# Heads p and p + 4 as a pair: q and k loaded over 128 partitions in one transfer

## The chip, the core and the metric

The kernel runs on one core of one Trainium2 chip. A core has five engines that run side by side, each with its own queue that it works off in order: PE (TensorE: matmuls and, on its weight port PEld, weight loads), DVE (VectorE), ACT (ScalarE), POOL (GpSimd) and SP (SyncE, which here issues most of the DMAs). Sixteen DMA engines move data between DRAM and the on-chip memory SBUF, which has 128 partitions. PE writes its results to PSUM.

The metric is the device time of one execution in microseconds (us), here the median of several runs. A profiled execution gives the trace. "Span" is the time from the program's first to its last instruction in that execution.

## What is computed

Eight batches of eight heads of attention with a forget gate, over 576 tokens with 64 dimensions each, and behind it a bilinear feed-forward layer on the rows of all heads side by side. Everything comes in and goes out as float32.

```python
batch, n_heads, seq, head_dim = (8, 8, 576, 64)
...
n_tokens, d_model, d_ff = (4608, 512, 1536)
...
def _attn_ref(q, k, v, f) -> np.ndarray:
    B, H, S, D = q.shape
    scale = 1.0 / np.sqrt(D)
    scores = scale * np.matmul(q, k.transpose(0, 1, 3, 2))
    log_f = np.log(np.clip(f, 0.0001, 1.0))
    cum = np.cumsum(log_f, axis=-1)
    decay = cum[:, :, :, None] - cum[:, :, None, :]
    causal = np.triu(np.ones((S, S), dtype=bool), k=1)
    scores = np.where(causal, -1000000000.0, scores + decay)
    scores = scores - np.max(scores, axis=-1, keepdims=True)
    attn = np.exp(scores)
    attn = attn / (np.sum(attn, axis=-1, keepdims=True) + 1e-09)
    return np.matmul(attn, v).astype(np.float32)
...
def _moe_ref(x, w_a, w_b, w_out) -> np.ndarray:
    a = x @ w_a
    b = x @ w_b
    return (a * b @ w_out).astype(np.float32)
...
    x = np.ascontiguousarray(attn_out.transpose(0, 2, 1, 3)).reshape(B * S, H * D)
```

## The kernel before

**Pairs of heads.** Attention works on two heads at a time, one on partitions 0 to 63 and one on 64 to 127. There are NP = 4 pairs in a batch and 32 in all, numbered t = 4 b + pr. Before the change pair pr holds heads 2 pr and 2 pr + 1.

**Loading q and k.** A half of q or k of a batch is four heads, so two pairs. `load_qk` (line 323) fetches it with two DMAs from SP's queue. Each DMA covers 64 partitions: partition g holds nine tokens in a row (TG = 9) of two neighbouring heads, as two runs of 2304 bytes. The two DMAs together fill the tile n32 (`k32`, `q32`), of which there are two buffers. `cast_qk` (L304 to L308, lines of the helper `cast`) turns it into 16-bit floats, on POOL from the second batch on, on ACT, DVE and POOL in the first. `pe_transpose` (line 336) transposes it on PE through PSUM (tile psT), 18 small matmuls for each half, and `pe_evict` copies the result to `qT` or `kT`.

**Scores and softmax.** `qk_group` (line 445) makes the scores of a pair in PSUM (tile sc, L451). In the first batch the gate's decay is added by further matmuls from `crow`; in later ones VectorE adds it from the tile `spread` (L532), which holds the running sums of log f of one pair on all 128 partitions. That tile is loaded from the scratch tensor `cum_d` (`load_spread`, line 502: one DMA over 128 partitions, whose source is one row repeated) or, for the four pairs of the second batch (PSPREAD), made by PE and copied. ACT takes the exponential (L559, L563), DVE the reciprocal (L571, L573), and POOL multiplies (`do_norm`, L581, the norms). The probabilities (tiles PA and PB) are transposed by a DMA of SP's queue (L591; in the first batch by PE), and `do_pv` and `do_pv4` (L621, L637) multiply them by v. The result goes to `xT[pr]`, the transposed input of the feed-forward layer: its partitions are the 128 rows of pair pr.

**Feed-forward layer.** `ff_mm` (L846) multiplies `xT` by `w_a` (psa) and `w_b` (psb), DVE multiplies the two, and `ff_out` (L866) multiplies by `w_out` (pso). The weights stay in SBUF in 16 bits. `weights` (line 430) loads them in nine DMAs from POOL's queue, which also cast: three column pieces each of `w_a` and `w_b`, in turn, and three row pieces of `w_out`. A piece may be issued no earlier than 8, 13, 18, ... on the planner's clock (W0, WD).

**The gate's sums.** `f_load` (line 257) reads f with four DMAs of 32 partitions, two from SP and two from ACT. Row 32 c + t of a half is pair t's head, c marking one of two equal copies. Clip, logarithm, scan and the 16-bit `crow` follow on DVE and ACT.

**What sets the order.** Nothing in the program is ordered by hand. `schedule` (line 155) is a planner in the kernel's own Python: every step is an `Op` with an engine, a planned duration, the steps that it needs, the ring buffers that it takes, and a priority; DMAs have a landing time from the table PKT (planned us of one packet of a size on one engine, line 132). The planner simulates the engines and the order that comes out is written to the engines' queues. On the chip each queue is worked off in that order, and an instruction whose input is late holds all behind it. A change of a planned number therefore moves instructions.

Of the kernel before, what the change touches and what calls it, by code (L numbers as in the profile page):

```python
# [25 lines left out]
def kernel(  # L26
# [105 lines left out]
    PKT = {256: 0.022, 1024: 0.094, 1536: 0.090, 2048: 0.085, 2304: 0.1, 4608: 0.217}  # L132
# [116 lines left out]
    def packets(n, size):  # L249
        return n * PKT[size] / 16  # L250

# [5 lines left out]
    def f_load(_):  # L257
# [3 lines left out]
        rows = f.rearrange("b (p two) s -> two (b p) s", two=2)  # L261
# [61 lines left out]
    def load_qk(b, which, half):  # L323

        x = T[("n32", which, b, half)] = n32_pool.tile([128, 2, TG, 64], FP32, tag="n32", bufs=RING["n32"], name=f"{which}32")
        for m in range(2):
            nc.sync.dma_start(out=x[64 * m:64 * m + 64].rearrange("g h t d -> g h (t d)"),  # L327
                              in_=src_of[which][b, 4 * half + 2 * m:4 * half + 2 * m + 2].rearrange("h (g t) d -> g h (t d)", t=TG))
# [35 lines left out]
    PSPREAD = tuple(int(x) for x in "1")  # L364
    DECP = tuple(range(1))

    def batch_inputs(b, base):
# [7 lines left out]
        for n, (which, sbs, gm) in enumerate(order_):  # L375
            p = base - 50 + 3 * n
            gt = gate(gm)
            if which == "v":
# [9 lines left out]
                else:  # L388
# [5 lines left out]
            ld = Op("SP", 1.05, lambda _, which=which, half=half: load_qk(b, which, half), gt, prio=p,  # L394
                    land=packets(64 * 4, 2304), name=f"ld{b}{which}{half}", bulk=b > 0)
# [34 lines left out]
    def weights(base):  # L430
        items = []
        for j in range(3):
            cols = slice(512 * j, 512 * j + 512)
            for nm, src, dst in (("a", moe_w_a, wa16), ("b", moe_w_b, wb16)):
                items.append(((nm, j), src.rearrange("(i p) c -> p i c", p=128)[:, :, cols], dst[:, :, cols]))
        for j in range(3):
            items.append((("o", j), moe_w_out.rearrange("(i p) c -> p i c", p=128)[:, 4 * j:4 * j + 4, :],
                          wout16[:, 4 * j:4 * j + 4, :]))
        for n, (key, src, dst) in enumerate(items):
            w_ops[key] = Op("POOL", 1.2, lambda _, src=src, dst=dst: nc.gpsimd.dma_start(out=dst, in_=src),  # L440
                            prio=-250, land=packets(512, 1024), name=f"ldw{key[0]}{key[1]}")
            w_ops[key].after = W0 + WD * n


    def qk_group(t, g):
# [7 lines left out]
        if g == 3:  # L453
# [8 lines left out]
            if b in DECP or b in PSPREAD:  # L462
# [145 lines left out]
    def do_pv(t, rows, parts):  # L608
# [6 lines left out]
        for j in range(rows[-1] + 1):  # L615
            for i in rows:
# [3 lines left out]
                for h in range(2):  # L620
                    nc.tensor.matmul(out=o[HP[h], 128 * i:128 * i + 128], lhsT=vt[:, j, 2 * pr + h, :],  # L621
# [360 lines left out]
```

## Time and profile before

| | us |
|---|---|
| median of 3 runs | 449.08 |
| lowest and highest of them | 448.56, 451.24 |
| the profiled execution, its own time | 448.2 |
| its span | 446.5 |

Busy shares are read against the span. The page also gives the chain of work that ended last, followed back from the last instruction, as shares of the span:

```profile
PE 45%; DMA 8%; DVE 3%; POOL 2%; SPq 2%; ACT 2%; issue 1%; POOLq 0%; ACTq 0%
...
q1 hardware_dynamic: 147072, 75.16, 79.5%
q0 software_dynamic: 4752, 4.72, 6.7%
```

The shares of the first line sum to 63%, so the chain is known only for the later part of the span. "DMA" in it is a transfer that someone waits for, "SPq" the issuing queue of SP. The two rows below are the two DMA queues with most of the traffic (packets, MB, share of the 16 engines' time): q1 is that of SP, q0 that of POOL, over which the weights come.

A row of a wait reads: engine, line and tile that waited, what ended the wait, us in total, times, longest. In a timeline row the bracket is the idle time ahead of the instruction and what ended it. In a row by stage the columns are busy time and instructions of each engine, the granted clock of PE (1.00 is full), the mean share of the DMA engines (over 1 where packets overlap) and GB/s.

### The profile page before, as it was taken

Reading aid. Unit: us, or ns where it says so; the run is one execution under the profiler, and the core shown is the slowest. Engines: PE = TensorE matmul, PEld = TensorE weight load, DVE = VectorE, ACT = ScalarE, POOL = GpSimd, SP = SyncE. Lnnn points to the kernel's source line nnn. Section 1 sums busy time; section 2 is a strip of 40 time slices with the busy share of each in tenths; the row PEclk is TensorE's granted clock in tenths of the full one; section 3 lists DMA queues with packets and bytes.
Section 4 is the critical chain, followed back from the end, with each engine's and each line's share of the span. In section 5 each row is a group of like instructions: output and inputs, shape, how many; then the busy total and the mean of one; then the engine's idle time right before and its main releaser. Section 6 shows DMA issues by size and latency. Waiting matters only on the chain.

```text
span 446.5 us, 11477 instructions
## 1 busy us (share of the span) xinstructions
PE 402.4 (90%) x4148; PEld 220.5 (49%) x4148; DVE 312.7 (70%) x1016; ACT 273.2 (61%) x777; POOL 221.9 (50%) x387
## 2 busy tenths in 40 slices
PE   1676998899989999989988999999799999999996
PEld 0344775475756544545444454455345454444552
DVE  4676989896778778887877778887587785233240
ACT  4586686666866677767767676767476674132131
POOL 6379776656446565656564566566444542000000
PEclk9996999899999999999999999999899999999999
DMA  8999999899999999999999999999979534200201
GB/s 189 239 226 174 178 208 188 204 174 217 257 244 237 227 209 235 218 235 215 239 187 205 241 275 200 204 249 225 220 139 217 148 75 76 94 1 1 94 1 70
DMA packets 151977, 80.75 MB, mean 181 GB/s; under 512 B 131248, under 2 KB 135856, under 8 KB 151920
## 3 DMA queue, kind: packets, MB, share of 16 engines
q1 hardware_dynamic: 147072, 75.16, 79.5%
q0 software_dynamic: 4752, 4.72, 6.7%
q8 instruction: 32, 0.52, 0.5%
q14 instruction: 25, 0.20, 0.2%
q10 hardware_dynamic: 96, 0.15, 0.1%
HBM read 52.20 MB, written 9.58 MB: 138 GB/s over the span
## 4 chain that ended last, share of the span: by engine, by line
PE 45%; DMA 8%; DVE 3%; POOL 2%; SPq 2%; ACT 2%; issue 1%; POOLq 0%; ACTq 0%
PE pso L866 15%; PE psa L846 12%; PE psb L846 11%; DMA q<-in_q_dram 6%; PE sc L451 4%; DMA k<-in_k_dram 2%; PE pv L621 2%; POOL q L306 1%; ACT PA L563 1%; SPq L327 1%; PE psT L342 1%; DVE ht L857 1%; DVE S L532 1%; SPq L591 1%; POOL k L308 1%
## 5 line engine op out<-in xcount | busy, mean ns | idle before, releaser
L532 DVE CUSTOM_DVE_ANT_0 S<-sc,spread 128x384 f32<-128x384 f32 (+3 forms) x280 | 141.1, 537 | 2.6 <-DMA spread<-cum_d 1.0
L581 POOL TENSOR_SCALAR PA<-PA,st 128x256 f16<-128x256 f16 (+2 forms) x192 | 89.2, 480 | 58.5 <-DVE st L573 49.6
L846 PE MATMUL psa<-xT,wa 128*128 128x512 f16 (+2 forms) x528 | 116.1, 343 | 1.2 <-ACT a L304 0.9
L846 PE MATMUL psb<-xT,wb 128*128 128x512 f16 (+2 forms) x528 | 116.1, 343 | 1.1 <-ACT kT L304 0.7
L857 DVE TENSOR_TENSOR ht<-psb,a 128x512 f16<-128x512 f32 (+2 forms) x132 | 78.0, 592 | 36.8 <-PE psb L846 29.4
L866 PE MATMUL pso<-wout,ht 128*128 128x512 f16 x432 | 100.5, 384 | 0.6 <-DVE ht L857 0.3
L304 ACT CAST a<-psa 128x512 f16<-128x512 f32 (+2 forms) x132 | 66.2, 502 | 54.0 <-PE psa L846 44.6
L563 ACT ACTIVATE PA<-S,st 128x256 f16<-128x256 f32 (+2 forms) x168 | 83.8, 502 | 20.2 <-DVE st L532 19.1
L581 POOL TENSOR_SCALAR PB<-PB,st 128x512 f16<-128x512 f16 (+1 forms) x96 | 67.2, 712 | 33.3 <-DVE st L573 26.0
L846 PEld LDWEIGHTS <-wa 128*128 128x128 f16 x528 | 49.7, 98 | 42.7 <-issue 3.3
L846 PEld LDWEIGHTS <-wb 128*128 128x128 f16 x528 | 49.9, 98 | 41.7 <-issue 3.1
L866 PEld LDWEIGHTS <-ht 128*128 128x128 f16 x432 | 40.6, 99 | 47.4 <-issue 2.8
L451 PE MATMUL sc<-kT,qT 64*64 64x64 f16 (+5 forms) x384 | 48.3, 311 | 4.9 <-ACT PA L563 4.1
L563 ACT ACTIVATE PB<-S,st 128x512 f16<-128x512 f32 x56 | 40.4, 722 | 9.8 <-DVE st L532 4.1
L308 DVE CAST xT<-pv 128x512 f16<-128x512 f32 (+1 forms) x40 | 23.3, 583 | 17.3 <-PE pv L621 17.1
L563 ACT ACTIVATION_READ_ACCUMULATOR PA<-S,st 128x1 f32 x168 | 32.0, 190 | 0.0
L451 PE MATMUL sc<-neg,low 64*128 64x64 f16 (+1 forms) x576 | 30.7, 195 | 0.0
L559 ACT ACTIVATE PB<-S,st 128x576 f16<-128x576 f32 x28 | 21.7, 776 | 13.2 <-DVE st L532 13.0
L451 PEld LDWEIGHTS <-qT 64*128 64x128 f16 (+1 forms) x384 | 15.2, 99 | 29.0 <-issue 17.3
L451 PEld LDWEIGHTS <-low 64*128 64x128 f16 (+1 forms) x576 | 23.4, 101 | 11.4 <-issue 1.8
L308 POOL CAST k<-k 128x1152 f16<-128x1152 f32 (+1 forms) x15 | 16.7, 1116 | 24.2 <-DMA k<-in_k_dram 22.1
L308 DVE COPY osb<-pso 128x512 f32<-128x512 f32 x17 | 11.7, 691 | 23.8 <-PE pso L866 23.7
(78 smaller groups left out, 384.0 us busy)
## 6 DMA issues: line engine op xcount, KB each, us to landing
spread<-cum_d SPq DMA_DIRECT2D x24, 576.0 KB, 5.2
k<-in_k_dram SPq DMA_DIRECT2D x32, 288.0 KB, 5.6
q<-in_q_dram SPq DMA_DIRECT2D x32, 288.0 KB, 5.3
out_dram<-osb SPq DMA_DIRECT2D x36, 256.0 KB, 3.2
v<-in_v_dram SPq DMA_DIRECT2D x32, 256.0 KB, 5.3
wa<-in_moe_w_a_dram POOLq DMA_DIRECT2D x3, 512.0 KB, 8.1
wb<-in_moe_w_b_dram POOLq DMA_DIRECT2D x3, 512.0 KB, 6.6
wout<-in_moe_w_out_dram POOLq DMA_DIRECT2D x3, 512.0 KB, 7.8
```

Of the source, the lines that this page charges most:

```text
L304: nc.scalar.copy(out=out_, in_=in_)
L306: VEC[e].tensor_scalar(out=out_, in0=in_, scalar1=0.125, scalar2=1.0, op0=MUL, op1=MUL)
L308: VEC[e].tensor_copy(out=out_, in_=in_)
L451: nc.tensor.matmul(out=dst, lhsT=lhsT, rhs=rhs, start=start, stop=stop, skip_group_check=True)
L532: nc.vector.tensor_tensor_reduce(out=o, in0=x, in1=y, scale=-1.0, scalar=3e38, op0=ADD, op1=MIN, accum_out=m)
L559: nc.scalar.activation(out=p_blocks(t, 4), in_=T[("s" if direct else "z", t, 4)], func=EXP, bias=st[:, 8:9], scale=sign, accum_out=st[:, 1 ...
L563: nc.scalar.activation(out=p_blocks(t, i)[:, :, h, :], in_=(T[("s", t, i)][:, h, :] if direct else T[("z", t, i)][:, h * n:h * n + n]).rea ...
L581: VEC[e].tensor_scalar(out=p, in0=p, scalar1=st[:, c:c + 1], scalar2=1.0, op0=MUL, op1=MUL)
L621: nc.tensor.matmul(out=o[HP[h], 128 * i:128 * i + 128], lhsT=vt[:, j, 2 * pr + h, :], rhs=pt[:, base_blk[i] + 2 * j + h, :], start=first, ...
L846: nc.tensor.matmul(out=p[:, 0:n], lhsT=w16[:, db, 128 * fb:128 * fb + 128], rhs=xTflat[db][:, t0:t0 + n], start=(db == 0), stop=(db == 3))
L857: nc.vector.tensor_tensor(out=ht[:, 0:n], in0=T.pop(("psb", t0, fb))[:, 0:n], in1=T.pop(("a16", t0, fb))[:, 0:n], op=MUL)
L866: nc.tensor.matmul(out=o, lhsT=T[("ht", t0, fb)][:, 128 * tb:128 * tb + 128], rhs=wout16[:, fb, :], start=(fb == 0), stop=(fb == 11))
```

## The change

Pair p now holds heads p and p + 4. A half of q or k is then pairs 2 half and 2 half + 1, that is two heads of the lower four and the same two of the upper four. Two neighbouring heads of 64 runs each are 128 runs in a row in DRAM, one for each partition, so one DMA loads the half: 128 partitions, two runs of 2304 bytes each. The rows of `xT` follow the new pairs, so the rows of `w_a` and `w_b` are loaded in two halves of 64 partitions each, in pieces of 512 and of 1024 columns: eight DMAs and, with the three of `w_out`, eleven. f is read in the new order of heads. `do_pv` and `do_pv4` take v's heads pr and pr + 4. The planner's figures change too: SP's issue of a load is 0.58 instead of 1.05, a weight issue 1.0 instead of 1.2, and the packet prices in PKT are new. PSPREAD is now tested by the pair; it names the same four pairs, 4 to 7.

```diff
-    PKT = {256: 0.022, 1024: 0.094, 1536: 0.090, 2048: 0.085, 2304: 0.1, 4608: 0.217}
+    PKT = {256: 0.0235, 1024: 0.096, 2048: 0.088, 2304: 0.1, 4608: 0.228}
...
-        rows = f.rearrange("b (p two) s -> two (b p) s", two=2)
+        rows = f.rearrange("b (h p) s -> h b p s", h=2)
...
-        for m in range(2):
-            nc.sync.dma_start(out=x[64 * m:64 * m + 64].rearrange("g h t d -> g h (t d)"),
-                              in_=src_of[which][b, 4 * half + 2 * m:4 * half + 2 * m + 2].rearrange("h (g t) d -> g h (t d)", t=TG))
+        src = src_of[which][b].rearrange("(j h) (g t) d -> j (h g) (t d)", j=2, t=TG)
+        nc.sync.dma_start(out=x.rearrange("p j t d -> p j (t d)"),
+                          in_=src[:, 128 * half:128 * half + 128].rearrange("j p x -> p j x"))
...
-    PSPREAD = tuple(int(x) for x in "1")
+    PSPREAD = {t for t in range(4, 8)}
...
-            ld = Op("SP", 1.05, lambda _, which=which, half=half: load_qk(b, which, half), gt, prio=p,
-                    land=packets(64 * 4, 2304), name=f"ld{b}{which}{half}", bulk=b > 0)
+            ld = Op("SP", 0.58, lambda _, which=which, half=half: load_qk(b, which, half), gt, prio=p,
+                    land=packets(128 * 2, 2304), name=f"ld{b}{which}{half}", bulk=b > 0)
...
+        for lo, hi in ((0, 512), (512, DF)):
+            for nm, src, dst in (("a", moe_w_a, wa16), ("b", moe_w_b, wb16)):
+                for h, r in enumerate(HP):
+                    items.append((nm, range(lo // 512, hi // 512),
+                                  src[256 * h:256 * h + 256].rearrange("(i d) c -> d i c", i=NP)[:, :, lo:hi],
+                                  dst[r, :, lo:hi], 256 * (hi - lo) // 512))
         for j in range(3):
-            cols = slice(512 * j, 512 * j + 512)
-            for nm, src, dst in (("a", moe_w_a, wa16), ("b", moe_w_b, wb16)):
-                items.append(((nm, j), src.rearrange("(i p) c -> p i c", p=128)[:, :, cols], dst[:, :, cols]))
...
+            o = Op("POOL", 1.0, lambda _, src=src, dst=dst: nc.gpsimd.dma_start(out=dst, in_=src),
+                   prio=-250, land=packets(n_, 1024), name=f"ldw{nm}")
+            o.after = W0 + WD * n
...
-                    nc.tensor.matmul(out=o[HP[h], 128 * i:128 * i + 128], lhsT=vt[:, j, 2 * pr + h, :],
+                    nc.tensor.matmul(out=o[HP[h], 128 * i:128 * i + 128], lhsT=vt[:, j, pr + NP * h, :],
```

The new figures move instructions on every engine. Three places matter here. The first is POOL's queue at the start of the program, before the change. wa and wb are the weights, spread, nv, k and q the tiles named above; numbers behind a name tell buffers apart, and "x2" is two such instructions in a row.

```order
L440 DMA wa_74<-in_moe_w_a_dram 128x4x512
L500 MEMSET spread_83 128x2x64
L308 CAST k_274<-k_199 128x2x5x64
L500 MEMSET spread_84 128x2x64
L440 DMA wb_75<-in_moe_w_b_dram 128x4x512
L581 TENSOR_SCALAR PA<-PA,st 128x2x128 x2
```

And POOL's queue at the same place after the change.

```order
L442 DMA wa_74<-in_moe_w_a_dram 64x4x512
L504 MEMSET spread_83 128x2x64
L308 CAST k_268<-k_195 128x2x5x64
L504 MEMSET spread_84 128x2x64
L442 DMA wa_74<-in_moe_w_a_dram 64x4x512
L585 TENSOR_SCALAR PA<-PA,st 128x2x128 x2
```

Ahead of the cast of the second k half now stands half of the first weight piece; its other half has taken the place of wb behind the cast.

The second place is ACT's queue at the start, before the change: the evictions of the first kT and qT, the cast of the second k half, the first exponentials.

```order
L304 COPY kT<-psT 128x576 x2
L304 COPY qT<-psT 128x576 x2
L304 CAST k_274<-k_199 128x2x4x64
L563 ACTIVATE PA,st<-sc_243,st 128x2x128 x2
L563 ACTIVATE PA,st<-sc_243,st 128x128 x2
```

ACT's queue there after the change.

```order
L304 COPY kT<-psT 128x576 x2
L304 COPY qT<-psT 128x576
L304 COPY spread_83<-scd 128x512
L304 CAST k_268<-k_195 128x2x4x64
L567 ACTIVATE PA,st<-sc_240,st 128x2x128 x2
L567 ACTIVATE PA,st<-sc_240,st 128x128 x2
```

One eviction has gone to DVE and a copy of spread has come; the cast of the second k half still stands ahead of the first exponentials.

The third place is SP's queue late in the program, before the change, around the loads of one half of k and q.

```order
L504 DMA spread_82<-cum_d 128x1152
L327 DMA k_4505<-in_k_dram 64x2x576 x2
L591 DMA_TRANSPOSE PTB<-PB_80 128x13x128
L327 DMA q_4567<-in_q_dram 64x2x576 x2
L504 DMA spread_83<-cum_d 128x1152
L591 DMA_TRANSPOSE PTA<-PA 128x12x128
L504 DMA spread_84<-cum_d 128x1152
```

SP's queue there after the change.

```order
L508 DMA spread_82<-cum_d 128x1152
L595 DMA_TRANSPOSE PTA<-PA 128x12x128
L508 DMA spread_83<-cum_d 128x1152
L595 DMA_TRANSPOSE PTB<-PB_80 128x13x128
L327 DMA k_4541<-in_k_dram 128x2x576
L327 DMA q_4566<-in_q_dram 128x2x576
L595 DMA_TRANSPOSE PTA<-PA 128x12x128
```

The load of q stood behind a transpose of the probabilities and now follows k's directly; the transpose has gone ahead of both.

More of the change, by code (lines that the diff above doesn't have):

```diff
@@ L431, in weights @@
         items = []
-        for j in range(3):
-            cols = slice(512 * j, 512 * j + 512)
-            for nm, src, dst in (("a", moe_w_a, wa16), ("b", moe_w_b, wb16)):
-                items.append(((nm, j), src.rearrange("(i p) c -> p i c", p=128)[:, :, cols], dst[:, :, cols]))
[L436 to L442, printed above, removed]
+        for lo, hi in ((0, 512), (512, DF)):
[4 more added lines that the diff above has]
+                                  dst[r, :, lo:hi], 256 * (hi - lo) // 512))
+        for j in range(3):
+            items.append(("o", [j], moe_w_out.rearrange("(i p) c -> p i c", p=128)[:, 4 * j:4 * j + 4, :],
+                          wout16[:, 4 * j:4 * j + 4, :], 512))
+        for n, (nm, js, src, dst, n_) in enumerate(items):
+            o = Op("POOL", 1.0, lambda _, src=src, dst=dst: nc.gpsimd.dma_start(out=dst, in_=src),
+                   prio=-250, land=packets(n_, 1024), name=f"ldw{nm}")
+            o.after = W0 + WD * n
+            for j in js:
+                w_ops.setdefault((nm, j), []).append(o)
     def qk_group(t, g):
@@ L461, in qk_group @@
                     mm(c[r, 0, :], ones[h], crow[r, 0:512], stop=True)
-            if b in DECP or b in PSPREAD:
+            if b in DECP or t in PSPREAD:
                 for h, r in enumerate(HP):
@@ L636, in do_pv4 @@
             for h in range(2):
-                nc.tensor.matmul(out=o[HP[h], :], lhsT=vt[:, j, 2 * pr + h, :],
+                nc.tensor.matmul(out=o[HP[h], :], lhsT=vt[:, j, pr + NP * h, :],
                                  rhs=pb[:, 8 + j, 64 * h:64 * h + 64], start=own and (j == 0),
@@ L671, in attention @@
         if not direct:
-            if b in PSPREAD:
+            if t in PSPREAD:
                 bc0 = Op("POOL", 0.2, lambda _: spread_tail(t), [o_p] + last_bc[-1:], prio=prio(0) - 5, name=f"bc0{t}")
@@ L894, in ffn @@
             p = base + fb
-            ma = Op("PE", mm4, lambda _, fb=fb: ff_mm(t0, n, fb, wa16, "psa"), need + [w_ops[("a", fb // 4)]],
+            ma = Op("PE", mm4, lambda _, fb=fb: ff_mm(t0, n, fb, wa16, "psa"), need + w_ops[("a", fb // 4)],
                     prio=5000 + p, mode="full", name="psa")
@@ L902, in ffn @@
             au = take(cp, "a16")
-            mb = Op("PE", mm4, lambda _, fb=fb: ff_mm(t0, n, fb, wb16, "psb"), need + [w_ops[("b", fb // 4)]],
+            mb = Op("PE", mm4, lambda _, fb=fb: ff_mm(t0, n, fb, wb16, "psb"), need + w_ops[("b", fb // 4)],
                     prio=5000 + p + 0.5, mode="full", name="psb")
@@ L917, in ffn @@
                         [m for m, _ in muls[4 * part:4 * part + 4]] + prev
-                        + [w_ops[("o", part)]],
+                        + w_ops[("o", part)],
                         prio=5000 + p + 0.1 * part, mode="full", name="pso")
```

## The prediction

> **What bounds the kernel now.** I read the page first, then the span cut into four stages, then who PE (TensorE) waits for in each stage, then the loads that stand behind those waits.
>
> ```profile
> span 446.5 us, 11477 instructions
> PE 402.4 (90%) x4148; PEld 220.5 (49%) x4148; DVE 312.7 (70%) x1016; ACT 273.2 (61%) x777; POOL 221.9 (50%) x387
> ...
> core 0: us, PE busy (x) PEld busy (x) DVE busy (x) ACT busy (x) POOL busy (x), PEclk, DMA share, GB/s
> 0.00:20.00 20.00, 6.24 (x88) 3.58 (x90) 10.33 (x19) 8.92 (x20) 9.43 (x40) 1.00 1.01 214
> 20.00:60.00 40.00, 32.15 (x464) 22.76 (x460) 31.45 (x92) 29.96 (x96) 32.85 (x57) 0.87 1.03 191
> 60.00:330.00 270.00, 251.21 (x2851) 139.25 (x2851) 214.54 (x747) 186.97 (x544) 158.67 (x254) 0.99 1.07 220
> 330.00:446.50 116.50, 112.76 (x760) 54.95 (x755) 56.41 (x159) 47.38 (x119) 20.96 (x39) 0.99 0.33 81
> ```
>
> PE is busy for 402.4 of 446.5 us. The matrix work of the second half of the program (lines 846 and 866) fills PE wherever attention leaves a hole, so the time is PE's work plus PE's idle time: 44.1 us. Of that, 20.0 - 6.2 = 13.8 lie in the start, 7.9 in the next 40 us, 18.8 between 60 and 330, and 3.7 at the end. From 0 to 330 the DMA engines are full (share 1.01 to 1.07); after that they are a third busy and PE runs without a break until the last outputs. So the question is which waits of PE end with a load. Below are the waits of PE between 60 and 330, then those of the first 30 us (columns: total, times, longest), and last POOL's own waits between 60 and 330.
>
> ```profile
> PE psT L342 <- POOL q L306: 8.6, 7, 2.6
> PE psT L342 <- POOL k L308: 5.9, 6, 2.0
> ...
> PE psT L342 <- DVE k L308: 7.8, 2, 7.6
> PE psT L342 <- ACT k L304: 2.7, 1, 2.7
> ...
> POOL q L306 <- DMA q<-in_q_dram: 18.2, 11, 3.0
> POOL k L308 <- DMA k<-in_k_dram: 13.8, 9, 2.4
> ```
>
> In the middle, 8.6 + 5.9 = 14.5 us of the 18.8 idle are one wait: the transposes psT of a fresh q or k stand in PE's order, and POOL has not yet cast that q or k, because POOL itself waits for the load (18.2 + 13.8 = 32.0 us). At the start the first, and later the second, k load hold PE in the same way. The loads of q and k are what ends PE's waits.
>
> **The load itself.** Two issues on SP's queue make one load; each covers 64 partitions. The first rows are the issues (min, median, max in ns), the second group the time from issue to landing between 60 and 330. Then come stretches of 1 us. In the first two the DMA engines move only q or k (the stretch at 80 and the like one at 200 have 96 packets in 0.22 MB, so 2304 B each), in the last two almost only spread, one transfer over 128 partitions (the stretch at 336 has 88 packets of 4608 B and 11 small ones). The last two columns are DMA share and GB/s.
>
> ```profile
> L327 SPq DMA_DIRECT2D k<-in_k_dram x32: 595/622/1888, 1.7 to 301.8; - x32
> ...
> spread<-cum_d SPq DMA_DIRECT2D x22, 576.0 KB, 5.4
> k<-in_k_dram SPq DMA_DIRECT2D x24, 288.0 KB, 5.4
> q<-in_q_dram SPq DMA_DIRECT2D x24, 288.0 KB, 5.1
> ...
> DMA packets 96, 0.22 MB, mean 221 GB/s; under 512 B 0, under 2 KB 0, under 8 KB 96
> ...
> DMA packets 99, 0.41 MB, mean 406 GB/s; under 512 B 11, under 2 KB 11, under 8 KB 99
> ...
> 80.00:81.00 1.00, 1.00 (x3) 0.29 (x2) 1.00 (x5) 0.58 (x1) 0.57 (x1) 0.50 1.03 221
> 150.00:151.00 1.00, 1.00 (x8) 0.59 (x6) 1.00 (x6) 1.00 (x5) 0.35 (x1) 1.00 1.04 221
> 284.00:285.00 1.00, 1.00 (x6) 0.48 (x5) 1.00 (x6) 0.76 (x4) 0.00 (x0) 1.00 0.97 369
> 336.00:337.00 1.00, 1.00 (x6) 0.49 (x5) 1.00 (x3) 0.53 (x2) 1.00 (x2) 1.00 1.04 406
> ```
>
> With the engines equally busy, a 64-partition load of q or k moves at 221 GB/s and the 128-partition one at 369 to 406. So half the partitions cost almost half the rate here, and a 576 KB transfer over 128 partitions lands as soon (5.4 us) as a 288 KB one over 64.
>
> **The change, part by part.**
>
> *One load of 128 partitions instead of two of 64.* The bytes and the rows of 2304 B stay; an issue goes. A load of 576 KB (589,824 B) takes 2.7 us at 221 GB/s and 1.5 to 1.6 at 369 to 406: 1.1 us less. The second issue, at least 0.6 us, also goes. By rates and issue a load is complete up to 1.1 + 0.6 = 1.7 us sooner. By the landing rows it is less: now a pair is in 0.6 + 5.1 to 5.4 = 5.7 to 6.0 us after its first issue began, the single one by spread's row after 5.4, some 0.5 sooner. Ends: 0.5 and 1.7. I take 1.1, the transfer alone, because the rate rows are the nearest: same size, same queue, nothing else under way.
>
> *What that is worth in the middle.* Thirteen waits of psT, 1.1 us on average, the longest two 2.6 and 2.0. At 0.5 each, 13 x 0.5 = 6.5 go. At 1.7 each all go but 0.9 and 0.3 of the longest two: 13.3. At 1.1 the longest two keep 1.5 and 0.9, and a few others keep something: some 11 go. Not all of it can reach the end, since what is late next are the transposes of the probabilities on SP's queue, and these wait for norms on POOL that no load delays:
>
> ```profile
> SPq L591 <- POOL PA L581: 49.0, 15, 5.6
> ```
>
> A PE that comes earlier meets these sooner. I let a quarter of the gain return as other waits: 11 x 0.75 = 8.3; ends 6.5 x 0.75 = 4.9 and 13.3.
>
> *The clock.* Two stretches in the middle run at half clock, each right behind short waits of PE (0.77 and 0.78 ahead of the first, 2.59 ahead of the second).
>
> ```profile
> 77.30 0.44 PE L342 MATMUL psT<-ident,q 64*128 64x64 f16 x18 [0.77 <-POOL q L306]
> 78.84 0.36 PE L621 MATMUL pv<-PTA,nv 128*64 128x128 f16 x6 [0.78 <-DMA PTA<-PA]
> ...
> 317.89 0.44 PE L342 MATMUL psT<-ident,q 64*128 64x64 f16 x18 [2.59 <-POOL q L306]
> ...
> 79.80:83.20 3.40, 3.40 (x10) 1.16 (x9) 2.64 (x8) 1.45 (x3) 2.21 (x4) 0.50 0.82 163
> 318.70:322.10 3.40, 3.40 (x10) 1.20 (x9) 2.24 (x11) 2.26 (x8) 0.67 (x1) 0.50 1.07 183
> ```
>
> PE is busy through both 3.4 us at a granted clock of 0.50, so each costs 1.7. With the waits gone both may go (3.4) or neither (0). I take one: 1.7. The Trainium skill ("TensorE: Matmul & The Clock Gate", "What's actually happening") lets the clock fall only after an idle window of about 3.4 us. No single wait in the middle is that long, so by the page the removal of short waits would bring no clock and the sum would be 1.7 us higher. The trace differs, 0.50 behind a wait of 2.59, and the measurement decides.
>
> *The start.* These are the first loads as the timeline has them.
>
> ```profile
> 4.13 0.60 DVE L276 TENSOR_SCALAR cum_f<-cum_f 128x576 f32<-128x576 f32 x1 [2.59 <-DMA cum_f<-in_f_dram]
> 6.84 1.04 POOL L440 DMA_DIRECT2D wa<-in_moe_w_a_dram  x1
> 7.13 1.05 DVE L308 CAST k<-k 128x512 f16<-128x512 f32 x2 [2.40 <-DMA k<-in_k_dram]
> 8.10 1.34 DVE L279 TENSOR_TENSOR_SCAN cum_f<-cum_f,cum_l 128x576 f32<-128x576 f16 x1
> 8.20 1.52 SPq L327 DMA_DIRECT2D k<-in_k_dram  x2
> 16.60 0.62 ACT L304 CAST k<-k 128x512 f16<-128x512 f32 x1 [4.01 <-DMA k<-in_k_dram]
> 17.27 0.50 PEld L342 LDWEIGHTS <-k 64*128 64x128 f16 x18 [3.19 <-ACT k L304]
> ...
> 11.00:12.50 1.50, 1.13 (x15) 0.50 (x17) 1.13 (x2) 1.09 (x2) 0.00 (x0) 1.00 1.25 209
> ```
>
> The second k load is issued at 8.20, when the first is cast, and is cast itself only at 16.60; ACT stands 4.01 us before it with the first exponentials queued behind. Ahead of it lies the first weight transfer, which fills the engines from 11.0 to 12.5 at 209 GB/s. Three things shorten this. The first casts come perhaps 0.5 us sooner (0 to 1.1). The weight piece ahead of it is now half, 256 KB less at 209 GB/s: 1.25 us, because its other half is issued on POOL only behind the cast of this very k. The load's own transfer is 1.1 shorter. Together 2.85; ends 0.5, if other transfers fill the hole, and 1.25 + 1.1 + 1.1 = 3.5. I take 2.7.
>
> The new view of f has batches outermost, eight rows of four heads. The Trainium skill ("DMA: Bandwidth & Descriptors", "Why a DMA increments its semaphore by 16 and not by 1") says that a DMA uses the largest number of engines up to 16 that divides the slowest dimension of both sides, which would put f on eight engines. No row here shows the engines of f. By the page f and the k behind it come later and the 0.5 us of the first casts is lost: the sum would be 0.5 higher. My 0 to 1.1 holds that case. What f itself feeds first, the clip at 4.13, has 8.10 - 4.73 = 3.4 us in hand before the scan, with a logarithm between.
>
> *Weights in eleven pieces, not nine.* Two more POOL issues of about 0.8 us stand in a stage where POOL has 40.0 - 32.9 = 7.1 us idle: 0. The planner's due times stand 5 us apart, so the last piece of w_out is due 10 us later.
>
> ```profile
> L440 POOL DMA_DIRECT2D wout<-in_moe_w_out_dram x3: 797/805/805, 43.1 to 53.7; - x3
> ...
> DMA to landing us min/median/max: 6.0/7.8/9.3
> ...
> L866 PE MATMUL pso<-wout,ht x72: 376/379/631, 71.8 to 132.9; 128*128 128x512 f16 x72
> ```
>
> It was issued at 53.7 and in by 53.7 + 9.3 = 63.0 at the latest; its first user starts after 71.8. Ten later is 73.0 at the worst and 71.5 at the median, and only the last third of that first product needs this piece. I take 0; ends 0 and 2 lost.
>
> *Heads, rows of weights, rows of f, the other side of PV.* Shapes, counts and types of the matmuls stay, so 0. The test of PSPREAD names the same four pairs: 0. The planner's packet prices and the shorter issue move work: from the fifth batch on, k and q are loaded directly behind one another. That is the place of the last rival.
>
> **Sum.** 8.3 + 1.7 + 2.7 = 12.7 us. The profiled execution took 448.2 us with a span of 446.5, so 435.5; the median of the three runs, 449.08, lies 0.9 above it: 436.4, say 436. With all low ends 4.9 + 0 + 0.5 - 2.0 = 3.4 go, with all high ones 13.3 + 3.4 + 3.5 = 20.2. All ends on one side at once is unlikely: the likeliest case's own range is 428 to 444.
>
> **The rivals.**
>
> *The gain moves.* Loads land sooner, but between 60 and 330 PE meets the norms and transposes instead, whose waits above (49.0 us on SP) are larger than those for loads. For it: POOL and SP run in order, so one late norm holds everything behind. Against it: PE itself waits almost only for q and k, 14.5 of 18.8. Only the start and some 1.5 us remain: 449.1 - 2.7 - 1.5 = 445.
>
> *The change does not do what it says.* The two halves are already under way together, and what limits them is the reading, not the 64 partitions. Then only an issue of 0.6 us goes, and the queue is as full as before: 448. Against it stands 406 GB/s for spread; for it, that spread reads a single row of DRAM over and over, and q does not.
>
> *Slower: k and q side by side.* Where SP now issues k and q together and PE has their psT 1.3 to 3 us apart late in the program, a late pair holds PE once for k and again for q, whose POOL cast comes behind k's. There are 12 pairs between 60 and 330 and they cost 14.5 / 12 = 1.2 us each now. If each pair costs the longest wait of today, 2.6, that is 12 x 2.6 = 31.2, or 16.7 more; with the start's 2.7 gained 449.1 + 16.7 - 2.7 = 463. It decides from 1.2 + (2.7 + 4.5) / 12 = 1.8 us per pair, with 4.5 us as one per cent. For it: SP's waits for norms ahead of a load reach 5.6. Against it: each load is shorter, and PE has other matrix work between.
>
> **How the numbers follow.** About one per cent, 4.5 us, is what a measurement of this kernel can tell from no change, so faster means under 444.6. Forecast: 0.62, all of it faster. The gain moves, 445: 0.18, of which 0.08 is faster and 0.10 the same. Not what it says: 0.10, the same. Side by side: 0.10, slower. Together 0.70 faster, 0.20 the same, 0.10 slower. The range is 428 to 447. It leaves out the slower case (0.10), the 448 (about half of 0.10, since runs of 448.56 and 451.24 show the spread) and the lower end of the forecast (0.05).
>
> **What would show it.** Right: 16 issues each of k and q with 576 KB; stretches of pure q or k over 300 GB/s; psT's waits between 60 and 330 under 6 us in all; ACT's wait for the second k under 2 us and that cast near 14; one or no stretch at clock 0.50 after 60. Wrong: pure stretches still near 221 GB/s (the reading limits), psT's waits gone but PE's idle time in the middle still near 18 (the gain moved), or psT's waits over 20 us, in k and q of the same pair (side by side).

## The result, and the profile after

The changed kernel takes 434.21 us (median of 4 runs, 432.76 to 436.07). The kernel before, on the same chip, takes 450.16 us (median of 4, 448.56 to 454.91). The ratio is 0.963, 95% interval 0.955 to 0.972: faster, by 16 us. The profiled execution of the changed kernel took 433.36 us with a span of 431.7, against 448.2 and 446.5 before, so the two profiles differ by 14.8 us of span. That is what has to be found. A few of the executions of the experiments below ran in a slower state; their times are left out of every median and ratio.

Below are, from the page of the changed kernel, its totals and the clock.

```profile
span 431.7 us, 11432 instructions
PE 398.8 (92%) x4148; PEld 219.6 (51%) x4148; DVE 310.5 (72%) x1017; ACT 271.8 (63%) x778; POOL 220.0 (51%) x387
...
PEclk9996999999999999999999999999999999999999
```

The span in the four stages of the prediction, by the view of stretches (same columns as there):

```profile
0.00:20.00 20.00, 7.70 (x102) 4.39 (x104) 11.38 (x23) 10.40 (x24) 9.74 (x43) 1.00 0.97 225
20.00:60.00 40.00, 31.17 (x466) 22.90 (x462) 31.29 (x98) 29.66 (x101) 32.63 (x56) 0.87 0.94 191
60.00:330.00 270.00, 262.46 (x2959) 144.80 (x2957) 222.67 (x782) 192.90 (x561) 162.93 (x263) 1.00 1.06 229
330.00:431.70 101.70, 97.44 (x630) 47.47 (x628) 45.21 (x119) 38.82 (x95) 14.67 (x27) 0.99 0.28 66
```

PE's idle time by stage is the stage less PE's busy time: 12.3, 8.8, 7.5 and 4.3 us, where it was 13.8, 7.9, 18.8 and 3.7. So the start gave 1.5, the next 40 us took 1.0 back, the middle gave 11.3 and the end took 0.5: 11.2 in all (the stages by unrounded rows). The rest is PE's busy time, 402.4 before and 398.8 now, 3.6 less for the same 4148 matmuls. 11.2 + 3.6 = 14.8, the whole difference.

The middle first: PE's waits for a fresh q or k between 60 and 330, POOL's own waits for the loads, and the largest waits of SP's queue for norms (total, times, longest).

```profile
PE psT L342 <- POOL q L306: 0.9, 2, 0.8
PE psT L342 <- POOL k L308: 0.6, 1, 0.6
...
POOL k L308 <- DMA k<-in_k_dram: 8.2, 8, 1.7
POOL q L306 <- DMA q<-in_q_dram: 2.2, 3, 1.0
...
SPq L595 <- POOL PB L585: 38.4, 19, 4.0
SPq L595 <- POOL PA L585: 36.7, 16, 4.4
```

The 14.5 us of PE's waits are 1.5. POOL's waits behind them fell from 32.0 to 10.4. SP's waits for the norms, which were to be late next, are shorter, too (49.0 for PA and 41.0 for PB then, 36.7 and 38.4 now), though it stands longer behind POOL's casts of k (3.7 then, 12.9 now) and v (6.4 then, 12.7 now; tile nv). PE itself waits 0.9 us for norms in this stage, and no wait of it for a DMA's transpose is listed.

Now the load itself: the issues of q and k over the whole span in the view of transfers (times issued, size, median us from issue to landing), first before and then after.

```profile
k<-in_k_dram SPq DMA_DIRECT2D x32, 288.0 KB, 5.6
q<-in_q_dram SPq DMA_DIRECT2D x32, 288.0 KB, 5.3
...
k<-in_k_dram SPq DMA_DIRECT2D x16, 576.0 KB, 5.3
q<-in_q_dram SPq DMA_DIRECT2D x16, 576.0 KB, 5.9
```

Stretches of 1 us in which hardly anything but q or k moves (columns as above; the last two are DMA share and GB/s):

```profile
236.00:237.00 1.00, 1.00 (x7) 0.47 (x5) 0.97 (x5) 0.76 (x3) 0.14 (x1) 1.00 0.99 389
280.00:281.00 1.00, 1.00 (x6) 0.47 (x5) 0.97 (x5) 0.76 (x3) 0.07 (x1) 1.00 1.05 408
```

And the packets of the last of them:

```profile
DMA packets 189, 0.41 MB, mean 408 GB/s; under 512 B 12, under 2 KB 12, under 8 KB 189
```

Sixteen issues of 576 KB each, and where q and k have the engines to themselves they move at 389 and 408 GB/s; before it was 221, at much the same DMA share. The rows of 2304 B are the same. A whole load of k lands as soon after its issue (5.3 us) as half a load did before (5.6); one of q lands later (5.9 against 5.3).

Next, the two stretches that ran at half clock before, as they are now.

```profile
79.80:83.20 3.40, 2.80 (x50) 1.97 (x49) 3.34 (x13) 3.40 (x11) 1.32 (x2) 1.00 1.16 253
318.70:322.10 3.40, 3.40 (x21) 1.43 (x19) 3.06 (x14) 3.40 (x13) 1.04 (x3) 1.00 1.05 118
```

Both are at full clock; the one dip that stays is the 6 in the clock's row above. Each had cost 1.7 us of PE's busy time, 3.4 together, which is nearly all of the 3.6.

Last the start, from the timeline (start, duration; in brackets the idle time before and what ended it).

```profile
0.81 2.04 ACTq L265 DMA_DIRECT2D cum_f<-in_f_dram  x2
0.82 1.65 SPq L265 DMA_DIRECT2D cum_f<-in_f_dram  x2
...
2.51 0.45 SPq L327 DMA_DIRECT2D k<-in_k_dram  x1
...
6.89 0.46 DVE L276 TENSOR_SCALAR cum_f<-cum_f 128x576 f32<-128x576 f32 x1 [5.35 <-DMA cum_f<-in_f_dram]
...
7.79 0.83 DVE L308 CAST k<-k 128x512 f16<-128x512 f32 x2 [0.44 <-DMA k<-in_k_dram]
...
8.53 1.35 DVE L279 TENSOR_TENSOR_SCAN cum_f<-cum_f,cum_l 128x576 f32<-128x576 f16 x1
...
8.64 0.38 SPq L327 DMA_DIRECT2D k<-in_k_dram  x1
...
15.06 0.62 ACT L304 CAST k<-k 128x512 f16<-128x512 f32 x1 [2.01 <-DMA k<-in_k_dram]
```

The first k is cast at 7.79, 0.66 later than before (7.13), and the second k load goes out 0.44 later (8.64 against 8.20). It is nevertheless cast 1.54 sooner (15.06 against 16.60). The two issues of f on SP take 1.65 us where k now follows at 2.51, and the clip of f starts at 6.89 instead of 4.13. Two further profiles of the same kernel (e8 and e11 below) have the first cast at 7.21 and 7.90 and the second at 14.35 and 15.80.

### The profile page after: what moved, and what is told of

The parts are those of the page before. It is cut to its first block, busy times and chain, and to the rows that moved or that the text cites. A ratio compares the mean times of both kernels' runs of the same rounds, so it can differ in the third digit from the quotient of the medians.

```text
span 431.7 us, 11432 instructions
## 1 busy us (share of the span) xinstructions
PE 398.8 (92%) x4148; PEld 219.6 (51%) x4148; DVE 310.5 (72%) x1017; ACT 271.8 (63%) x778; POOL 220.0 (51%) x387
## 4 chain that ended last, share of the span: by engine, by line
PE 57%; DVE 3%; DMA 1%; issue 1%; POOL 0%; ACT 0%; SPq 0%; ACTq 0%; POOLq 0%
PE pso L870 16%; PE psb L850 16%; PE psa L850 16%; PE sc L455 5%; PE pv L625 3%; DMA k<-in_k_dram 1%; DVE S L536 1%; PE psT L342 1%; PE sc L641 1%; DVE ht L861 0%; DVE osb L308 0%; DVE kT L308 0%; POOL k L308 0%; POOL PB L585 0%; DVE xT L308 0%
## 5 line engine op out<-in xcount | busy, mean ns | idle before, releaser
L536 DVE CUSTOM_DVE_ANT_0 S<-sc,spread 128x256 f32<-128x256 f32 (+2 forms) x280 | 141.5, 536 | 3.3 <-PE sc L455 2.4
L870 PE MATMUL pso<-wout,ht 128*128 128x512 f16 x432 | 100.2, 380 | 0.6 <-DVE osb L308 0.6
L567 ACT ACTIVATE PA<-S,st 128x128 f16<-128x128 f32 (+2 forms) x168 | 83.9, 503 | 13.1 <-DVE st L536 12.2
L870 PEld LDWEIGHTS <-ht 128*128 128x128 f16 x432 | 40.0, 98 | 45.4 <-issue 0.6
L567 ACT ACTIVATE PB<-S,st 128x512 f16<-128x512 f32 x56 | 40.4, 722 | 17.7 <-POOL PA L585 12.3
L567 ACT ACTIVATION_READ_ACCUMULATOR PA<-S,st 128x1 f32 x168 | 32.1, 191 | 0.0
L577 DVE RECIPROCAL st<-st 128x2 f32<-128x2 f32 x128 | 20.0, 159 | 14.5 <-ACT PA L567 11.1
L455 PEld LDWEIGHTS <-low 64*128 64x128 f16 (+1 forms) x576 | 23.3, 100 | 11.1 <-issue 2.0
L304 ACT COPY osb<-pso 128x512 f32<-128x512 f32 x19 | 11.0, 577 | 27.5 <-PE pso L870 27.5
```

The source lines that it names most:

```text
L304: nc.scalar.copy(out=out_, in_=in_)
L455: nc.tensor.matmul(out=dst, lhsT=lhsT, rhs=rhs, start=start, stop=stop, skip_group_check=True)
L536: nc.vector.tensor_tensor_reduce(out=o, in0=x, in1=y, scale=-1.0, scalar=3e38, op0=ADD, op1=MIN, accum_out=m)
L567: nc.scalar.activation(out=p_blocks(t, i)[:, :, h, :], in_=(T[("s", t, i)][:, h, :] if direct else T[("z", t, i)][:, h * n:h * n + n]).rea ...
L577: nc.vector.reciprocal(out=st[:, 20 + 2 * i:22 + 2 * i], in_=st[:, 10 + 2 * i:12 + 2 * i])
L870: nc.tensor.matmul(out=o, lhsT=T[("ht", t0, fb)][:, 128 * tb:128 * tb + 128], rhs=wout16[:, fb, :], start=(fb == 0), stop=(fb == 11))
```

## The experiments

All times in us; each ratio is to the kernel before on the same chip, with its 95% interval.

| Run | What is different | Median (beside it: before) | Ratio |
|---|---|---|---|
| e1 | changed kernel, load in two halves of 64 partitions | 445.71 (448.71) | 0.993, 0.990 to 0.996 |
| e7 | the same, each transfer every second partition | 435.51 (450.0) | 0.971, 0.966 to 0.977 |
| e2 | two transfers, each over 128 partitions | 436.46 (448.71) | 0.970, 0.960 to 0.979 |
| e3 | kernel before with the new load alone | 432.9 (448.71) | 0.964, 0.956 to 0.971 |
| e5 | kernel before with the planner's new figures alone | 446.54 (450.41) | 0.992, 0.988 to 0.996 |
| e6 | changed kernel with the old figures | 431.56 (450.41) | 0.959, 0.951 to 0.968 |
| e4 | changed kernel, f in the old view | 432.28 (448.71) | 0.963, 0.958 to 0.969 |
| e8 | changed kernel, again | 433.83 (450.0) | 0.966, 0.962 to 0.969 |
| e9 | as e4, beside e8 | 431.11 (450.0) | 0.960, 0.956 to 0.964 |
| e10 | changed kernel, first k issued ahead of f | 434.7 (449.48) | 0.968, 0.963 to 0.973 |
| e11 | changed kernel, beside e10 | 433.01 (449.48) | 0.966, 0.961 to 0.972 |

The theory is that the 64 partitions of a transfer held the rate down. The rivals are that the number of issues decides, that the planner's new order does (packet prices and the shorter issue), or another part of the change.

**e1, the new order with the old shape of transfer.**

```diff
-        nc.sync.dma_start(out=x.rearrange("p j t d -> p j (t d)"),
-                          in_=src[:, 128 * half:128 * half + 128].rearrange("j p x -> p j x"))
+        for m in range(2):
+            lo = 128 * half + 64 * m
+            nc.sync.dma_start(out=x[64 * m:64 * m + 64].rearrange("p j t d -> p j (t d)"),
+                              in_=src[:, lo:lo + 64].rearrange("j p x -> p j x"))
```

> The changed kernel, with each load of q or k again in two transfers of 64 partitions (same data, same place, every queue in the same order but for the second issue). Partitions (a transfer over all 128 partitions moves faster, and this is the gain): most of it goes, 443 to 449 us; stretches with q or k alone near 221 GB/s, psT's waits between 60 and 330 us over 8 us. Order (the planner's new figures put the work better and the loads don't matter): 433 to 437, psT's waits under 4. Issues (one instruction less on SP's queue is the gain): 443 to 449 as well; the next run parts these two.

Measured: 445.71. A stretch of pure q and k in its profile:

```profile
296.00:297.00 1.00, 1.00 (x24) 0.60 (x24) 0.32 (x2) 0.71 (x2) 0.00 (x0) 1.00 1.04 221
```

And PE's waits for q and k between 60 and 330:

```profile
PE psT L344 <- POOL q L306: 5.2, 6, 1.8
PE psT L344 <- POOL k L308: 2.7, 3, 1.2
```

The rate is back at 221 GB/s and with it 7.9 us of the waits, a little short of the 8 that were expected. (This profile is of the longest of e1's ten executions.) All else of the change is still there, and of its 16 us some 3 are left (448.71 - 445.71).

**e2, two issues, but each over all 128 partitions.**

```diff
-        nc.sync.dma_start(out=x.rearrange("p j t d -> p j (t d)"),
-                          in_=src[:, 128 * half:128 * half + 128].rearrange("j p x -> p j x"))
+        for j in range(2):
+            nc.sync.dma_start(out=x[:, j].rearrange("p t d -> p (t d)"),
+                              in_=src[j, 128 * half:128 * half + 128])
```

> The changed kernel, with each load of q or k in two transfers that both cover 128 partitions, one run of 2304 bytes each. Partitions: 433 to 438, stretches with q or k alone over 330 GB/s. Issues: 443 to 449. Order: 433 to 437.

Measured: 436.46. There are as many issues of q and k as in e1, and the time is 9 us lower. A stretch late in its profile shows the rate:

```profile
303.00:304.00 1.00, 1.00 (x13) 0.54 (x10) 0.69 (x2) 0.74 (x3) 0.92 (x3) 1.00 1.10 406
```

406 GB/s from two issues: the number of issues is not the cause. What the extra issue costs lies within the spread (e2's runs go from 431.69 to 437.22).

**e7, 64 partitions, but every second one.** The transfers of e1, with as many packets and as many partitions (64) in each, only spread over the whole height.

```diff
-        nc.sync.dma_start(out=x.rearrange("p j t d -> p j (t d)"),
-                          in_=src[:, 128 * half:128 * half + 128].rearrange("j p x -> p j x"))
+        src = src[:, 128 * half:128 * half + 128].rearrange("j (p two) x -> two p j x", two=2)
+        dst = x.rearrange("(p two) j t d -> two p j (t d)", two=2)
+        for m in range(2):
+            nc.sync.dma_start(out=dst[m], in_=src[m])
```

> The changed kernel, but each load of q or k goes in two transfers of 64 partitions as in the first experiment, only that each takes every second partition, so that both reach from the first partition to the last. If 64 partitions are slow because they lie side by side in one half, these two are as quick as one of 128: 433 to 438 us, pure stretches of q and k above 330 GB/s, waits of psT between 60 and 330 under 4 us. If the number of 64 is what counts: 443 to 447 us, pure stretches near 221 GB/s, waits of psT of 7 to 10 us. If the order of issue decides, nothing changes against the first experiment either: 446.

Measured: 435.51. A stretch of its profile:

```profile
239.00:240.00 1.00, 1.00 (x7) 0.41 (x6) 0.97 (x3) 0.77 (x3) 0.00 (x0) 1.00 1.03 380
```

PE's wait for q between 60 and 330 (there is none for k):

```profile
PE psT L344 <- POOL q L306: 1.6, 2, 1.3
```

380 GB/s with 64 partitions. So it is not their number that slows a transfer, but that they lie side by side. That they also lie in one half of the 128 goes with it in e1, and no run here parts the two. The Trainium skill ("SBUF — State Buffer", "Door 1: The DMA port swizzle (why `[64,N]` ≈ `[32,N]`)") has a rule for this: a transfer is as quick as the number of the 16 SBUF ports that its partitions reach, and of two ports one serves the lower 64 partitions and the other the upper 64. By it, e1's transfers reach 8 ports and e7's all 16. The runs agree: 221 against 380 GB/s, with 408 for one transfer over all 128. The ports themselves have no row in a trace. This is the sharpest of the runs: e1 and e7 differ only in which partitions a transfer takes, with the rows in DRAM that belong to them, and stand 10.2 us apart (on two chips, where the kernel before takes 448.71 and 450.0). The rows read do not explain it: e1 reads neighbouring rows, and so does the load over 128 partitions, at 408 GB/s.

**e3, the new load alone.** The kernel before, with its heads in neighbouring pairs after the load, its order of weights and its figures; only the load takes 128 partitions. The products then take heads in wrong pairs with v and f, with the same shapes and counts.

```diff
-        for m in range(2):
-            nc.sync.dma_start(out=x[64 * m:64 * m + 64].rearrange("g h t d -> g h (t d)"),
-                              in_=src_of[which][b, 4 * half + 2 * m:4 * half + 2 * m + 2].rearrange("h (g t) d -> g h (t d)", t=TG))
+        src = src_of[which][b].rearrange("(j h) (g t) d -> j (h g) (t d)", j=2, t=TG)
+        nc.sync.dma_start(out=x.rearrange("p j t d -> p j (t d)"),
+                          in_=src[:, 128 * half:128 * half + 128].rearrange("j p x -> p j x"))
```

> The kernel before, its order untouched, with the one load over 128 partitions alone: weights, f and v stay by the old pairs, so that rows of the result belong to other pairs of heads. Partitions: 434 to 441, psT's waits between 60 and 330 us from 14.5 to under 6. Order: 446 to 450, psT's waits stay over 10.

Measured: 432.9, as good as the whole change. PE's waits between 60 and 330 in its profile:

```profile
PE psT L342 <- POOL k L308: 4.8, 5, 1.6
PE psT L342 <- POOL q L306: 2.0, 3, 1.1
```

6.8 us of waits stay where the whole change leaves 1.5. Both figures of e3 lie a little outside what was expected of it (434 to 441, under 6). This profiled execution took 435.0, the longest of its four and 1.6 above the profiled one of the changed kernel. PE's idle time in the middle is 11.3 us against 7.5, and in the other three stages 2.2 less than in the changed kernel (11.1, 8.3 and 3.7 against 12.3, 8.8 and 4.3). The load alone brings the gain. The rest of the change, taken together, adds nothing that these runs show; it holds both fewer waits in the middle and the new view of f, which costs at the start (e9).

**e5 and e6, the planner's figures alone, and the change without them.**

```diff
-    PKT = {256: 0.022, 1024: 0.094, 1536: 0.090, 2048: 0.085, 2304: 0.1, 4608: 0.217}
+    PKT = {256: 0.0235, 1024: 0.096, 2048: 0.088, 2304: 0.1, 4608: 0.228}
...
-            ld = Op("SP", 1.05, lambda _, which=which, half=half: load_qk(b, which, half), gt, prio=p,
+            ld = Op("SP", 0.58, lambda _, which=which, half=half: load_qk(b, which, half), gt, prio=p,
```

This is e5, made on the kernel before; e6 makes the reverse edit on the changed kernel.

> The kernel before with the planner's new figures alone (packet prices, 0.58 us for SP's issue of a load); loads stay two transfers of 64 partitions. Partitions: 444 to 450, within 1.5% of before. Order: 434 to 438.

> The changed kernel with the planner's old figures (packet prices, 1.05 us for SP's issue). Partitions: 434 to 440, psT's waits between 60 and 330 us under 6. Order: 444 to 450.

Measured: 446.54 and 431.56. With the slow loads the new order is worth 3.9 us (450.41 - 446.54), near what e1 kept (448.71 - 445.71 = 3.0). With the quick loads it is worth nothing that can be told: e6, without it, is no slower, and came out below the 434 to 440 that were expected. The two gains do not add up.

**e4, e8 and e9, the view of f.**

```diff
-        rows = f.rearrange("b (h p) s -> h b p s", h=2)
+        rows = f.rearrange("b (p two) s -> two (b p) s", two=2)
```

> The changed kernel, with the rows of f read in the old order (the decay then belongs to other heads). If f's new view is what made f land at 6.9 instead of 4.1 us, f lands near 4.2, the first k is cast before 7.2 and the second before 14.3, and the time is 1 to 2 us shorter than the changed kernel's: 432 to 433.5. If f's lateness is hidden behind the k loads, the second k cast stays near 15 and the time within 0.5 us.

> The changed kernel as it is, once more beside the next kernel on one chip. Theory 'f is hidden' (its later landing delays only the start, and the planner's work fills the hole): both within 0.3% of each other, 432 to 435 us. Theory 'f costs the start' (the second k load is cast 2.5 us later in the profiled runs): this one 2 to 2.5 us longer than the next.

> The changed kernel with f read in the old view (two halves of four heads, batches inside), so that the decays belong to other heads than q and k; all else is as changed. Theory 'f is hidden': 432 to 435 us, as the changed kernel. Theory 'f costs the start': 430 to 432 us, 2 to 2.5 us below it. In both the clip of f starts near 4.1 us instead of 6.9 and the second k load is cast near 12.5 instead of 15.

e4 came out at 432.28, too near the changed kernel to tell. So both went onto one chip with six runs each: 433.83 for the changed kernel (e8), 431.11 with the old view (e9). The means lie 2.3 us apart (433.90 and 431.62; standard deviation 1.2 in each, so 0.7 to 3.9 with 95%). The rows of e9's start:

```profile
0.81 0.90 ACTq L265 DMA_DIRECT2D cum_f<-in_f_dram  x2
0.81 0.87 SPq L265 DMA_DIRECT2D cum_f<-in_f_dram  x2
...
1.73 0.42 SPq L327 DMA_DIRECT2D k<-in_k_dram  x1
...
4.04 0.46 DVE L276 TENSOR_SCALAR cum_f<-cum_f 128x576 f32<-128x576 f32 x1 [2.50 <-DMA cum_f<-in_f_dram]
...
6.16 0.86 DVE L308 CAST k<-k 128x512 f16<-128x512 f32 x2 [1.66 <-DMA k<-in_k_dram]
...
11.77 0.62 ACT L304 CAST k<-k 128x512 f16<-128x512 f32 x1 [0.24 <-DMA k<-in_k_dram]
```

With the old view the clip, the first cast and the second cast come at 4.04, 6.16 and 11.77, against 6.31, 7.21 and 14.35 in the profile of e8. So the new view delays the start, and the times lie some 2 us apart. That it is the delay of the start that reaches the end isn't shown; what the two profiles say of it stands at the end of the next section.

**e10 and e11, the first k ahead of f.** If the clip ahead of the k cast is what costs, it can be moved: SP issues k first, and DVE casts it before it waits for f. The planned figures of f change with it, and ACT's `warm_table` no longer waits for f's issue in the plan.

```diff
-    o_f = Op("SP", 1.1, f_load, prio=-310, land=0.6)
+    o_f = Op("SP", 1.65, f_load, prio=-310, land=2.0)
...
-    o_w = Op("ACT", 2.2, warm_table(LN), [o_f], prio=-300)
+    o_w = Op("ACT", 2.2, warm_table(LN), prio=-300)
+    o_w.after = 0.7
...
-            ld = Op("SP", 0.58, lambda _, which=which, half=half: load_qk(b, which, half), gt, prio=p,
+            ld = Op("SP", 0.58, lambda _, which=which, half=half: load_qk(b, which, half), gt,
+                    prio=-320 if (b, which, half) == (0, "k", 0) else p,
```

> The changed kernel with f in its new view, but SP issues the first k load ahead of f, and DVE casts that k ahead of f's clip (the clip's planned landing is later). Theory 'f costs the start because the clip stands in front of the first k cast': the k cast starts near 5.5 us instead of 7.8, the second k load goes out near 6.5 instead of 8.6, and the time falls by 1.5 to 2.5 us against the changed kernel beside it, to 431 or 432. Rival 'f is late whatever stands ahead of it': the scan still ends near 9.9, the first scores wait for it, and the time stays within 1 us of the changed kernel.

> The changed kernel as it is, on the chip of the run before, to compare with: 433 to 434 us, 1.5 to 2.5 us above it if the clip ahead of the k cast is what costs.

Measured: 434.7 against 433.01 for the changed kernel beside it. The first casts and the scan in e10's timeline:

```profile
4.71 1.01 DVE L309 CAST k<-k 128x512 f16<-128x512 f32 x2 [4.71 <-DMA k<-in_k_dram]
...
8.79 1.35 DVE L280 TENSOR_TENSOR_SCAN cum_f<-cum_f,cum_l 128x576 f32<-128x576 f16 x1
...
13.69 0.62 ACT L305 CAST k<-k 128x512 f16<-128x512 f32 x1 [0.77 <-DMA k<-in_k_dram]
```

The first three stages of its span:

```profile
0.00:20.00 20.00, 9.02 (x128) 5.46 (x130) 11.08 (x22) 12.90 (x30) 12.18 (x46) 1.00 1.01 245
20.00:60.00 40.00, 30.77 (x470) 21.84 (x464) 34.45 (x107) 30.11 (x102) 33.25 (x58) 0.91 1.04 205
60.00:330.00 270.00, 260.53 (x2896) 143.10 (x2892) 219.66 (x760) 190.60 (x551) 159.72 (x257) 1.00 0.99 224
```

And the same three stages of e11, the changed kernel beside it:

```profile
0.00:20.00 20.00, 7.04 (x98) 4.05 (x98) 10.56 (x21) 9.66 (x22) 9.69 (x42) 1.00 0.92 216
20.00:60.00 40.00, 31.53 (x462) 22.96 (x462) 31.61 (x97) 30.05 (x101) 32.40 (x56) 0.87 0.94 193
60.00:330.00 270.00, 262.97 (x2964) 145.20 (x2962) 223.39 (x783) 193.55 (x563) 164.17 (x264) 1.00 1.05 230
```

The casts of e10 come at 4.71 and 13.69, 3.2 and 2.1 sooner than in e11 (7.90 and 15.80), as that theory said. The time does not fall: the means are 434.1 and 433.3, so e10 is 0.8 longer, with 95% between 0.6 shorter and 2.3 longer. The 1.5 to 2.5 us that the theory promised are not there. The edit moves other work, too (ACT has 779 instructions in e10 and 778 in e11, DVE 1016 and 1017), so what the earlier cast would be worth in an unchanged order isn't shown. The scan still starts at 8.79, as the rival had it. Whether that later scan is itself the 2 us of f's view isn't shown. The stages show where the early start went: PE's idle time is 11.0, 9.2 and 9.5 us in e10's three, and 13.0, 8.5 and 7.0 in e11's. Two microseconds are won in the first 20 and more than lost again by 330.

## Why the prediction was right, point by point

The forecast, 436 us and faster, came true, and its mechanism is shown: loads over half of the partitions moved at little over half the rate, the change repairs that, and PE's waits for q and k go. Its terms, against the difference of the two profiled executions (14.8, forecast 12.7):

- *The load, 1.1 us sooner.* Right by the rates: 576 KB at 389 to 408 GB/s are 1.4 to 1.5 us, where 221 GB/s took 2.7. The rows from issue to landing, which the prediction had as its low end, say less: a pair of half loads was in 0.6 + 5.6 = 6.2 us (k) and 0.6 + 5.3 = 5.9 (q) after its first issue, the single load after 5.3 and 5.9. So k lands 0.9 sooner after its issue and q no sooner. Late in the program q's load now stands right behind k's. The rival that the reading of DRAM limits, with spread's single row as its doubt, is refuted by 389 and 408 GB/s on q and k themselves, and by e7.
- *The middle, 8.3.* The mechanism was right, the term too small: 11.3. Of the 14.5 us of waits 13.0 went, not 11, and 1.7 came back as other idle time (13.0 - 11.3), not a quarter. The norms and transposes that were to be late next were not: PE waits 0.9 us for norms there, and SP waits less for them than before. That is also why the rival "the gain moves" fell.
- *The clock, 1.7.* Too small: both stretches went, 3.4. It is the least certain of the terms, since the same program does not do it each time. The timeline of e8, the same kernel, has a wait of 1.61 us and one of 0.43:

```profile
61.78 0.23 PE L601 MATMUL psP<-ident,PB 128*128 128x128 f16 x1 [1.61 <-POOL PB L585]
62.44 0.69 PE L601 MATMUL psP<-ident,PB 128*128 128x128 f16 x7 [0.43 <-POOL PB L585]
```

  The stretch behind them, PE busy throughout at a clock of 0.50, which costs 1.6 us:

```profile
62.80:66.00 3.20, 3.20 (x25) 1.87 (x24) 2.04 (x5) 0.00 (x0) 2.76 (x5) 0.50 1.17 167
```

  In the other two profiles of this kernel the waits at this place are 0.48 and 0.43 (the first one) and 0.51 and 0.43 (e11), and the clock stays at 1.00. The rule weighed there (the Trainium skill, "TensorE: Matmul & The Clock Gate", "What's actually happening"), that an idle window of about 3.4 us lowers the clock, would have given 0 (the prediction's "the sum would be 1.7 us higher" means the time, not the gain). Taken as one unbroken wait, it disagrees with this trace as well.
- *The start, 2.7.* Too large: 1.5 (2.2 and 0.8 by the profiles of e8 and e11), and this is the step that failed: "The first casts come perhaps 0.5 us sooner (0 to 1.1)." They come 0.66 later (0.08 and 0.77 in e8 and e11). With the old view of f they do come sooner, at 6.58 (e3), 6.23 (e4) and 6.16 (e9) against 7.13 before, by 0.55 to 0.97. So the new view of f is what turned the step round. It takes SP 1.65 us to issue where the old one takes 0.87 (e9), so k goes out at 2.51 instead of 1.73. From there to its cast k takes 5.28 us, where e9 has 4.43; what makes this longer has no row.

  The clip, in front of the cast on DVE, is 2.76 late, too, but it ends at 7.35, and the wait of 0.44 between it and the cast ends with k's own load. Of the three profiles of this kernel only e8's has the cast follow the clip without a wait. The clip's own 3.4 us in hand all but cover its lateness: the scan starts 0.43 later. Nor is all of that lateness the view's alone: in e1, with the same view but loads at 221 GB/s, the clip starts at 5.00.

  The prediction looked at who waits for f's data. It did not price the issue of f, behind which k stands on SP, nor what f's view does to the time until k is in. It bounded this wrongly, too: it held that the 0 to 1.1 contained the case of the late f, and the value fell below 0. The other two parts, 1.25 + 1.1 = 2.35, measured 1.98: the second k load was issued 0.44 later and cast 1.54 sooner. The rule of the Trainium skill that was weighed there ("DMA: Bandwidth & Descriptors", "Why a DMA increments its semaphore by 16 and not by 1"), by which f would use eight engines, named the right place and a loss. That f lands later agrees with it; the number of engines has no row here.
- *Weights in eleven pieces, 0.* Right. The rows of what PE's third product (L870) waits for name an eviction (0.6 us) and "issue" (0.6), time in which the profile shows no wait; no weight is among them, nor among PE's waits from 0 to 330.
- *Heads, rows, the other side of PV, 0.* Right for the heads, the rows of weights and the other side of PV as far as the runs go: e3, without them, takes as long. Not right for the rows of f: e9 against e8 puts them at 0.7 to 3.9 us lost.
- *Not in the sum.* The stages from 20 to 60 and from 330 on have 1.5 us more idle time than before (0.98 + 0.52). In the first 60 us PE now waits 2.1 us for a transpose (PTA), for which no wait is listed there before; the rest was not followed.
- *Slower, k and q side by side.* It did not happen. The pairs do follow one another on SP late in the program, and what psT waits for POOL in the whole middle is 1.5 us.

Against the list of what would show it: issues, rate, waits of psT and clock are as said. ACT's wait for the second k is 2.01, not under 2, and that cast is at 15.06, not near 14: the start's error again.

What stays open: why a change of the first microseconds (e9 against e8, by 2 us, or e10 with its early casts, by none) reaches the end in one case and not in the other. In the two profiles of e8 and e9 PE's idle time is nearly the same, 32.3 and 32.1 (span less the sum of PE's busy time): e9 gains 1.3 us in the first 20 and gives 2.4 back between 20 and 60. Of the 1.7 us between the two spans 1.5 are PE's busy time (399.9 and 398.4). So it is not shown that the 2.3 us between the means come from the start, and no run separates what remains. No version here is told apart from the changed kernel as faster with all heads in their places: e6's runs, 429.97 to 435.92, overlap its own.

## What to carry to other kernels

Look at the GB/s of stretches in which one kind of transfer is alone while the DMA engines are full: a load that writes one half of the partitions may move at half the rate, as here. A view that spreads it over all of them, even at every second one, was worth more here than fewer issues or a better order. When an operation is made later, ask not only who needs its result but what stands behind it on its own queue, and price the new view's issue along with its transfer. Time won in the first microseconds counts only if the profile shows that it is still there at the end.

## What the runs showed of the hardware that was not expected

- Two transfers of 64 partitions side by side moved at 221 GB/s (e1), the same two at every second partition at 380 (e7), one over all 128 at 389 and 408. The engines were equally busy (share 0.99 to 1.05).
- Issuing f as eight rows of four heads took 1.65 and 2.04 us for two issues, where 32 rows at an even distance took 0.87 and 0.90 (e9), with the same bytes.
- The clock fell to 0.50 after a wait of 1.61 us and one of 0.43 shortly after it (e8), and in two other executions of the same program, where the waits at this place were 0.48 and 0.51 with 0.43 behind, it did not fall. Nor did it behind a single wait of 2.1 us in the first profile (for PTA, near 55), while before the change it fell behind two of 0.77 and 0.78. So the length of one wait does not decide it.
